# One written order for the whole kernel: q and k as nine tokens a partition, PSUM banks as single tiles, weight loads held to a place in the order

## The chip, the cores and the metric

The kernel runs on one core of a Trainium2 chip, in one launch. The metric is device time in microseconds (us). The kernel computes with TensorE (PE: matmuls and transposes, weight loads shown as PEld), VectorE (DVE), ScalarE (ACT) and GpSimd (POOL). DMAs are issued by SyncE's queue (SP), by POOL (where float32 is cast to fp16 on the way) and a few by ACT. Each engine and each queue takes its instructions strictly in program order.

## What is computed

There are 8 batches of 8 heads with 576 tokens of 64 channels. Each head has a coarse attention (q, k and v averaged over 4 tokens, 144 by 144 scores, output repeated 4 times) and a local one (each token sees the keys less than 4 tokens away). Their sum goes, as 4608 tokens by 512 channels, through a two-layer MLP with an ELU:

```python
out_up = np.repeat(out_d, factor, axis=2)            # coarse attention, factor 4
mask = np.abs(pos[:, None] - pos[None, :]) < factor  # local attention
out_local = np.matmul(attn, v)
x = (out_up + out_local) ...                         # [B * S, H * D] = [4608, 512]
h = x @ w_in                                         # 512 -> 2048
g = np.where(h > 0.0, h, np.exp(np.minimum(h, 0.0)) - 1.0)
return g @ w_out                                     # 2048 -> 512
```

## The kernel before

Attention goes by pairs of heads, 4 pairs (j) in each of 8 batches (b). The MLP goes by 9 blocks (t) of 512 tokens; a block has 64 matmuls of 128x512 for the first layer (`mm1`: 16 columns of blocks fc, 4 matmuls dc each, where dc is the pair of heads whose channels it reads) and 64 for the second (`mm2`). Block t needs the attention of batches up to t for t of 1 to 7, and block 0 needs batch 0 alone. So the kernel is a front (batch 0, the weights, batch 1), a long middle in which a batch of attention is worked in between the matmuls of the MLP, and an end of MLP alone.

- Loads: `load_qk` brings q and k of a pair as float32 on SP, on 96 partitions with 6 tokens each (two runs of 1536 bytes a partition); `load_cast` does it for batches 0 and 1 on POOL's queue. `load_v`/`load_windows` (L258, L280) bring v, from batch 1 on as four DMAs of 80 KB a pair in pieces of 256 bytes, into one of 3 buffers. `load_wi` (L172) and `load_wo` (L176) bring the weights in four DMAs each on POOL's queue.
- `cast_qk` (L242) and `cast_v` (L303) cast to fp16 on POOL. `transposes` (L324, L329) turn q, and in batches 0 to 2 k, by six transposes of 96x128 a tensor; from batch 3 on (`FLIP`) a DMA transpose turns k (L808). `evict_q`/`evict_k` (L359, L366) put the tokens in order; `sums` (L378 on DVE, L395 and L397 on POOL) makes the coarse q and k.
- `scores` and `coarse` (L459, L472), `exps` (L482), `mask` (L497), `denominators` (L519, L525); the reciprocals are spread over partitions by PE and a copy (L582, L592) in batches 0 to 2, and through DRAM after (`spread_out`, `spread_in`); `near_outputs`, `far_outputs` (L603, L623), `normalise` (L667, L672, L684).
- Batch 0 has a program of its own (`masked_scores`, `masked_exps`, `den_half`, `spread_half`, `outputs_half`, `normalise_half`): windows of 112 keys, a mask that is added through PE, coarse sums through PE, work in half batches. The first layer of block 0 runs in halves of 256 tokens (`mm1_part`, L699).
- `mm1` (L720), then `exp` on ACT (L724), `min(e,1)-1` (L725) and `max(h,0)+e` (L726) on DVE; `mm2` (L740), a copy on ACT (L746) and a store on SP (L748).
- PSUM has eight banks: two tiles of two banks for scores, outputs, spreads and transposes (a third one until `close_front`), two banks for `mm1`, two for the rest. `keep` issues idle matmuls on a zero tile (L759).

The order is a list of events sorted by a time written out by hand, in units of about one `mm1` column; all engines get their instructions in that one order. The numbers for the front stand in `F`, those for the batches in `PLAN`, and `MM1`/`MM2` place the MLP:

```python
for _, _, fn, args in sorted(events, key=lambda e: e[:2]):
    fn(*args)
```

Of the kernel before, what the change touches and what calls it, by code (L numbers as in the profile page):

```python
# [16 lines left out]
SD = S // 4  # L17
SH = SD // 2
SCALE = 0.125
QB, KW, NB, PAD = 96, 112, 6, 8  # L20
HB = 3 * QB
TPP = S // QB
# [5 lines left out]
RW = S + SD  # L28
KG, CG = 96, 24
KO = 16  # L30
# [5 lines left out]
I1 = 31  # L36


def _np_consts():

    f16 = np.float16
    off = np.arange(KW) - PAD
    m = np.zeros((KW, NB, QB), dtype=f16)
    for c in range(NB):
        for u in range(QB):
            ok = (np.abs(off - u) < 4) & (off + QB * c >= 0) & (off + QB * c < S)
            m[ok, c, u] = 1.0
    m = m.reshape(KW, S)
    neg = ((m - 1) * 30000).astype(f16)
    rs = np.zeros((QB, 3, SD), dtype=f16)  # L50
    for c in range(3):
        rs[np.arange(QB), c, (TPP * np.arange(QB) + 2 * c) // 4] = 0.25
    vr = np.zeros((KW, 32), dtype=f16)
    vr[PAD + np.arange(QB), np.arange(QB) // 4] = 0.25
    ind = np.zeros((KW, 190), dtype=f16)
    ind[:, I1] = 1.0
    ind[np.arange(KW) % 32 < CG, 63 + I1] = 1.0
    ind[:, 126:] = 1.0
    for n, z in enumerate((10, 5)):
        ind[:, 127 + 32 * n : 126 + 32 * n + z] = 0.0  # L60
    return np.eye(KW, dtype=f16), neg, rs.reshape(QB, 3 * SD), vr, ind


def _np_windows():
# [26 lines left out]
    return mask.reshape(128, WL), vr.reshape(128, 96), ind  # L91
# [12 lines left out]
def kernel(  # L104
# [11 lines left out]
    dr = ctx.enter_context(tc.tile_pool(name="dr", bufs=1, space=bass.MemoryType.DRAM))  # L116
    ctx.enter_context(nc.allow_low_precision("fp16 operands of TensorE"))
    ctx.enter_context(tc.manual_schedule())

    def const(a, name, queue):  # L120
        t = C[name] = sb.tile(list(a.shape), FP16, tag=name, bufs=1, name=name)
        queue.dma_start(out=t[:], in_=nc.inline_tensor(a, name=name + "c").ap())

    front = ctx.enter_context(ExitStack())
    ps = ctx.enter_context(tc.tile_pool(name="ps", bufs=1, space=bass.MemoryType.PSUM))
    fp = front.enter_context(tc.tile_pool(name="fp", bufs=1, space=bass.MemoryType.PSUM))
    late = {}

    def one(name, dt=FP32):
        return ps.tile([128, 512 if dt == FP32 else 1024], dt, tag="misc", bufs=2, name=name)  # L130

    turns = [0, 1, 2]

    def two(name, dt=FP32):

        turns.append(turns.pop(0))
        pool = fp if turns[-1] == 2 else ps
        return pool.tile([128, 1024 if dt == FP32 else 2048], dt, tag=f"two{turns[-1]}", bufs=1, name=name)

    def bank(tag, name):  # L140
        pool = late["ps"] if tag == "hp" else ps
        return pool.tile([128, 512], FP32, tag=tag, bufs=2, name=name)

    def close_front():
        front.close()
        turns.remove(2)
        late["ps"] = ctx.enter_context(
            tc.tile_pool(name="late", bufs=1, space=bass.MemoryType.PSUM)
        )

    def g2(ap, a, n):

        return _free(ap[:, a : a + 1], [[512, 2], [1, n]])
# [4 lines left out]
    id_np, neg_np, sums_np, vr_np, ind_np = _np_consts()  # L158
    mask_np, vr2_np, ind2_np = _np_windows()
    C = {}  # L160
    WI = sb.tile([128, DMC, DFF], FP16, tag="WI", bufs=1, name="WI")
    WO = sb.tile([128, FCN, DM], FP16, tag="WO", bufs=1, name="WO")
    KT = [sb.tile([128, S + 2 * KO], FP16, tag=f"kt{i}", bufs=1, name="kt") for i in range(4)]

    def w_in(dc, fc):

        a = 512 * (fc // 4) + fc % 4
        return WI[:, dc, a : a + 509 : 4]

    def load_wi(a, z):  # L170
        src = moe_w_in.rearrange("(c p) m -> p c m", p=128)[:, :, a:z]
        nc.gpsimd.dma_start(out=WI[:, :, a:z], in_=src)  # L172

    def load_wo(n):
        src = moe_w_out[512 * n : 512 * n + 512].rearrange("(p c) m -> p c m", c=4)
        nc.gpsimd.dma_start(out=WO[:, 4 * n : 4 * n + 4, :], in_=src)  # L176

    KD = [sb.tile([128, 2 * KG + 16], FP16, tag=f"kd{i}", bufs=1, name="kd") for i in range(4)]
    KE = [sb.tile([128, 192], FP16, tag=f"ke{i}", bufs=1, name="ke") for i in range(4)]
    QT = [sb.tile([128, S + 4], FP16, tag=f"qt{i}", bufs=1, name="qt") for i in range(4)]  # L180
    qk32, qk16, v32s, v16s = {}, {}, {}, {}
    st = {}

    def runs_of(src, b, j):

        a = src[b, 2 * j]
        return bass.AP(
            tensor=a.tensor, offset=a.offset, ap=[[TPP * D, QB], [S * D, 2], [1, TPP * D]]
        )

    def by_head(x):

        return x[:].rearrange("p c e d -> p (c e d)").rearrange("p (e n) -> p e n", e=2)

    def is_cast(b, j):

        return b < 2 and (b, j) != (0, 0)

    def load_cast(b, j):
        qk16[(b, j)] = []  # L200
        for src, name in ((q, "q16"), (k, "k16")):
            x = sb.tile([QB, NB, 2, D], FP16, tag=name, bufs=4, name=name)
            nc.gpsimd.dma_start(out=by_head(x), in_=runs_of(src, b, j))
            qk16[(b, j)].append(x)

    def load_qk(b, j, held=False):

        got = []
        for src, name in ((q, "q"), (k, "k")):
            a = src[b, 2 * j]  # L210
            t = sb.tile([QB, 2 * NB, D], FP32, tag=name + "32", bufs=3, name=name + "32")
            if held:
                nc.vector.memset(t[0:1, 0, 0:1], 0.0)
            runs_ = name == "q" or b < FLIP
            nc.sync.dma_start(
                out=t[:].rearrange("p (e r) d -> p e (r d)", e=2) if runs_ else t[:],
                in_=bass.AP(
                    tensor=a.tensor, offset=a.offset,
                    ap=[[TPP * D, QB], [S * D, 2], [1, TPP * D]] if runs_
                    else [[D, QB], [QB * D, 2 * NB], [1, D]],  # L220
                ),
            )
            got.append(t)
        qk32[(b, j)] = got

    AP_ = sb.tile([1, 1], FP16, tag="apart", bufs=1, name="apart")

    def apart(x):

        nc.gpsimd.tensor_copy(out=AP_[:], in_=x)  # L230

    def cast_qk(b, j, half=False):

        got = []
        for t, name in list(zip(qk32.pop((b, j)), ("q16", "k16")))[:: 1 if b < FLIP else -1]:
            x = sb.tile([QB, NB, 2, D], FP16, tag=name, bufs=4, name=name)
            src = t[:].rearrange("p (e c) d -> p c e d", e=2)
            if half:
                act(out=x[:, :, 0, :], in_=src[:, :, 0, :])
                dve(out=x[:, :, 1, :], in_=src[:, :, 1, :])  # L240
            else:
                nc.gpsimd.tensor_copy(out=x[:], in_=src)  # L242
                apart(x[0:1, 0, 0, 0:1])
            got.append(x)
        qk16[(b, j)] = got[:: 1 if b < FLIP else -1]

    V00 = sb.tile([KW, 2 * NB, D], FP32, tag="v32", bufs=3, name="v32")

    def load_v(b, j):

        a = v[b, 2 * j]
        if b:
            load_windows(b, j, a)
            return
        t = V00 if (b, j) == (0, 0) else sb.tile([KW, 2 * NB, D], FP32, tag="v32", bufs=3, name="v32")

        def part(p0, p1, i0, i1):
            nc.sync.dma_start(  # L258
                out=t[p0:p1, i0:i1, :],
                in_=bass.AP(  # L260
                    tensor=a.tensor, offset=a.offset + (QB * i0 - PAD + p0) * D,
                    ap=[[D, p1 - p0], [QB * D, i1 - i0], [1, D]],
                ),
            )

        if (b, j) == (0, 0):
            part(0, KW, 1, 2 * NB)
            part(PAD, KW, 0, 1)
        else:
            part(0, KW, 0, 2 * NB)  # L270
        v32s[(b, j)] = t

    def load_windows(b, j, a):

        t = sb.tile([128, 2 * WM, D], FP32, tag="v32", bufs=3, name="v32")
        if b == 1:
            nc.vector.memset(t[0:1, 1, 0:1], 0.0)

        def part(h, e, n=64, m0=0, m1=WM):
            nc.sync.dma_start(  # L280
                out=t[64 * h : 64 * h + n, WM * e + m0 : WM * e + m1, :],
                in_=bass.AP(
                    tensor=a.tensor, offset=a.offset + (WQ * h - 3 + S * e + 2 * WQ * m0) * D,
                    ap=[[D, n], [2 * WQ * D, m1 - m0], [1, D]],
                ),
            )

        last = (b, j) == (B - 1, NPAIR - 1)
        if last:
            nc.gpsimd.memset(t[96:128, 2 * WM - 1, :], 0.0)  # L290
# [756 lines left out]
```

## Time and profile before

| what | value |
| --- | --- |
| runs (3) | 350.78 us median, 350.11 to 354.14 |
| profiled execution, first to last instruction | 355.1 us |
| PE busy / weight loads | 336.1 / 185.5 us |
| DVE, ACT, POOL busy | 236.4, 180.3, 160.8 us |
| mean granted TensorE clock | 0.976 |
| HBM read, written | 41.97 MB, 9.55 MB |

The profiled execution is a little longer than the three timed runs. PE's busy time counts overlapping matmuls and PE's waits inside a pipelined group too, so it is not PE at its peak; what an instruction really takes of PE is read from the distance of its start to the next one's. The granted clock is the share of the full TensorE clock. DMA shares are sums of the times of packets over 16 engines, and can exceed 1 where packets overlap.

### The profile page before, as it was taken

To read this page: it belongs to the slowest core of one execution; us is meant where nothing else is said; L and a number is where in the kernel's file an instruction comes from. 1 tells how busy PE (TensorE), PEld (TensorE's weight loads), DVE (VectorE), ACT (ScalarE), POOL (GpSimd) and SP (SyncE) were. 2 spreads that over 40 slices of the span, in tenths; PEclk is the share of its full clock that TensorE was granted. 3 is DMA by queue.
4 is the path that set the end of the run, shared out by engine and by line. 5 is a ranking of instruction groups with operands and counts; after the bars stand their busy time and mean duration, and the time that the engine had idled before them with its cause. 6 is when DMAs were issued, how large, how long until landed. Compare 5 with 4: busy or idle time off the path is not lost.

```text
span 355.1 us, 10487 instructions
## 1 busy us (share of the span) xinstructions
PE 336.1 (95%) x4288; PEld 185.5 (52%) x4288; DVE 236.4 (67%) x466; ACT 180.3 (51%) x312; POOL 160.8 (45%) x298
## 2 busy tenths in 40 slices
PE   7993998799979999999999999999999999999996
PEld 3762885344545454545454555555455544444443
DVE  2334799566789877987697789768755855555510
ACT  4580587225755664466456645663553444444421
POOL 4464449279495834974397449855300500000000
PEclk9998799959999999999999999999999999999999
DMA  8999979997999698998979796943004010011012
GB/s 173 184 166 203 191 172 216 215 186 185 189 152 224 120 205 168 167 185 174 181 155 206 158 218 144 188 123 61 30 32 118 31 59 30 31 46 43 31 59 89
DMA packets 100304, 48.89 MB, mean 138 GB/s; under 512 B 81617, under 2 KB 95265, under 8 KB 100257
## 3 DMA queue, kind: packets, MB, share of 16 engines
q1 hardware_dynamic: 94417, 41.86, 57.8%
q0 software_dynamic: 5600, 6.26, 10.8%
q8 instruction: 33, 0.54, 0.7%
q10 hardware_dynamic: 240, 0.11, 0.2%
q14 instruction: 14, 0.11, 0.1%
HBM read 41.97 MB, written 9.55 MB: 145 GB/s over the span
## 4 chain that ended last, share of the span: by engine, by line
PE 72%; DMA 13%; DVE 6%; ACT 3%; issue 2%; POOL 2%; SPq 1%; DVEq 0%; POOLq 0%; ACTq 0%
PE op L740 31%; PE hp L720 28%; DMA v<-in_v_dram 6%; DMA rcb<-rd 3%; DMA WO<-in_moe_w_out_dram 3%; DVE ln L672 2%; PE sc L759 2%; PE tqk L329 2%; DMA rd<-rc 2%; PE lg L603 2%; DVE e L725 1%; PE sc L459 1%; ACT e L724 1%; DVE gt L726 1%; PE lg L623 1%
## 5 line engine op out<-in xcount | busy, mean ns | idle before, releaser
L740 PE MATMUL op<-WO,gt 128*128 128x512 f16 (+2 forms) x592 | 147.0, 377 | 1.0 <-DVE gt L726 0.6
L724 ACT ACTIVATE e<-hp 128x512 f16<-128x512 f32 x144 | 86.1, 599 | 110.5 <-PE hp L720 95.7
L720 PE MATMUL hp<-xt,WI 128*128 128x512 f16 x512 | 133.4, 384 | 0.7 <-DVE gt L726 0.5
L726 DVE SCALAR_TENSOR_TENSOR gt<-hp,e 128x512 f16<-128x512 f32 x144 | 99.6, 692 | 6.4
L725 DVE TENSOR_SCALAR e<-e 128x512 f16<-128x512 f16 x144 | 60.7, 421 | 58.1 <-ACT e L724 57.6
L740 PEld LDWEIGHTS <-gt 128*128 128x128 f16 x592 | 55.6, 98 | 62.8 <-issue 3.0
L720 PEld LDWEIGHTS <-WI 128*128 128x128 f16 x512 | 55.5, 115 | 49.6 <-issue 3.1
L684 POOL TENSOR_TENSOR xt<-ln 128x128 f16<-128x128 f16 (+7 forms) x55 | 36.7, 695 | 50.8 <-DVE ln L672 50.8
L482 ACT ACTIVATE pex<-sc 128x580 f16<-128x580 f32 (+1 forms) x56 | 30.2, 596 | 9.7 <-PE sc L472 9.7
L395 POOL TENSOR_TENSOR t<-qt 128x288 f32<-128x288 f16 x27 | 18.1, 671 | 36.8 <-ACT qt L359 36.8
L303 POOL CAST v<-v 128x640 f16<-128x640 f32 (+1 forms) x32 | 24.2, 756 | 21.1 <-DMA v<-in_v_dram 21.0
L746 ACT COPY os<-op 128x512 f32<-128x512 f32 (+2 forms) x37 | 21.4, 577 | 19.3 <-PE op L740 19.1
L378 DVE TENSOR_REDUCE ke<-kt 128x145 f16<-128x580 f16 x28 | 21.0, 751 | 2.4 <-ACT kt L366 2.4
L359 ACT COPY qt<-tqk 128x576 f16<-128x576 f16 x28 | 17.9, 638 | 8.5 <-PE tqk L329 6.7
L699 PE MATMUL hp<-xt,WI 128*128 128x256 f16 x128 | 17.3, 288 | 4.6 <-issue 4.6
L672 DVE TENSOR_TENSOR ln<-lg,rcb 128x580 f16<-128x580 f32 x28 | 21.1, 752 | 0.0
L242 POOL CAST q<-q 96x768 f16<-96x768 f32 x24 | 19.9, 828 | 0.0
L242 POOL CAST k<-k 96x768 f16<-96x768 f32 x24 | 19.8, 825 | 0.1
L699 PEld LDWEIGHTS <-WI 128*128 128x128 f16 x128 | 13.6, 118 | 5.8 <-issue 4.7
L497 DVE TENSOR_TENSOR pex<-pex,MASK 128x580 f16<-128x580 f16 x28 | 14.0, 500 | 3.8 <-ACT pex L482 3.6
L397 POOL TENSOR_TENSOR qd<-t 128x144 f16<-128x144 f32 x27 | 12.4, 461 | 2.1
L459 PEld LDWEIGHTS <-kt 64*64 64x64 f16 x560 | 7.0, 108 | 11.7 <-issue 8.8
(113 smaller groups left out, 271.6 us busy)
## 6 DMA issues: line engine op xcount, KB each, us to landing
out_dram<-os SPq DMA_DIRECT2D x35, 256.0 KB, 2.2
v<-in_v_dram SPq DMA_DIRECT2D x111, 80.0 KB, 4.6
q<-in_q_dram SPq DMA_DIRECT2D x25, 288.0 KB, 4.1
k<-in_k_dram SPq DMA_DIRECT2D x25, 288.0 KB, 5.1
rcb<-rd SPq DMA_DIRECT2D x10, 364.0 KB, 4.6
WI<-in_moe_w_in_dram POOLq DMA_DIRECT2D x4, 512.0 KB, 10.9
WO<-in_moe_w_out_dram POOLq DMA_DIRECT2D x4, 512.0 KB, 9.2
q<-in_q_dram POOLq DMA_DIRECT2D x7, 144.0 KB, 7.2
```

The lines of the kernel that those rows point to most:

```text
L242: nc.gpsimd.tensor_copy(out=x[:], in_=src)
L303: nc.gpsimd.tensor_copy(out=v16[:], in_=v32[:].rearrange("p (e c) d -> p c e d", e=2))
L482: nc.scalar.activation(out=s["p"][:, :, a : a + n], in_=g2(sc, a, n), func=AF.Exp, scale=SCALE / 16 if a else SCALE,)
L672: nc.vector.tensor_tensor(out=ln[:, 0 : 2 * WL].rearrange("p (m h u) -> p m h u", h=2, u=WQ), in0=_free(lg[:, 0:1], [[WQ, WM], [512, 2], [ ...
L684: eng.tensor_tensor(out=xt(t)[:, j, t0 - TBLK * t : t1 - TBLK * t], in0=ln[:, a:z], in1=_rep4(ln[:, ga : ga + (z - a) // 4]), op=AB.add,)
L699: nc.tensor.matmul(FS[i][:, 256 * f : 256 * f + 256], w_in(dc, 2 * n + f), xts[0][:, dc, 256 * h : 256 * h + 256], start=(f == dc == 0), s ...
L720: nc.tensor.matmul(hp, w_in(dc, fc), xts[t][:, dc, :], start=(dc == 0), stop=(dc == DMC - 1),)
L724: nc.scalar.activation(out=e, in_=hp, func=AF.Exp)
L725: nc.vector.tensor_scalar(out=e, in0=e, scalar1=1.0, scalar2=-1.0, op0=AB.min, op1=AB.add)
L726: nc.vector.scalar_tensor_tensor(out=to, in0=hp, scalar=0.0, op0=AB.max, in1=e, op1=AB.add)
L740: nc.tensor.matmul(op_[:, a:z], gts[t][:, fc, 128 * tt : 128 * tt + 128], WO[:, fc, a:z], start=(fc == 0), stop=(fc == FCN - 1),)
L746: nc.scalar.copy(out=os_[:, a:z], in_=op_[:, a:z])
```

## The change

The program is written anew. The order of everything is one string of 1730 words (`ORDER`), made by a list scheduler, and a word is a step with its numbers: which tensor, batch, pair, the engine (0 ACT, 1 DVE, 2 POOL, 4 SP) or the PSUM tile. All batches take the same path, so batch 0's own functions, their constants and the fourth kind of window go. In particular:

- q, and k where PE turns it, are loaded as one run of nine tokens (2304 bytes) on each of 128 partitions, and turned by 18 transposes of 64x64 a tensor (`t`) in place of six of 96x128. k by DMA transpose (`fl`) is as before.
- The four single PSUM banks (4 to 7) are tiles of their own, and any of them serves `mm1`, `mm2`, a turn, the v sums or the denominators as the order says; two tiles of two banks stay, the third is there until `close`.
- `min(e,1)` and `max(e-1, h)` replace `min(e,1)-1` and `max(h,0)+e`; in 28 of 144 columns ACT does the minimum by itself (`er` relu(-h), `ey` exp(-e)). 24 of the final adds (`ad`) go to DVE, most sums of k (`s.1`) go to POOL.
- `WI` is two tiles, loaded in four parts (half the columns, two dc each), `WO` four. `hw` writes one element of a weight tile on DVE, so that the load of it waits for that place in DVE's order; `hv` and `hx` do the same for the first loads of v, q and k into a buffer. v has 4 float32 buffers instead of 3.
- The first layer of block 0 runs over all 512 tokens, matmul by matmul as a pair is ready (`m.t.fc.d0.d1.bank`).

```diff
+    def load_x(x, b, j, eng):
+        src = bass.AP(tensor=a.tensor, offset=a.offset, ap=[[NINE * D, 128], [1, NINE * D]])
...
+    def hold_w(n, eng):
+        engines[eng].memset((WI[0][0:1, 0, 0:1], WO[0][0:1, 0, 0:1])[n], 0.0)
...
+    def load_wi(n, i, eng):
+        src = moe_w_in.rearrange("(c p) m -> p c m", p=128)
+        queues[eng].dma_start(
+            out=WI[n][:, 2 * i : 2 * i + 2, :], in_=src[:, 2 * i : 2 * i + 2, 1024 * n : 1024 * n + 1024]
+        )
...
+    def turn(x, b, j, p):
+        src, to = nth((Q16, K16)[x], b, j), bank(p).bitcast(FP16)
+        for c in range(NINE):
+            for e in range(2):
+                r = heads(e)
+                nc.tensor.transpose(to[r, 64 * c : 64 * c + 64], src[r, 64 * c : 64 * c + 64], ID[r, r])
...
+    def elu_min(t, fc, eng):
+        e = e_of(t, fc)
+        engines[eng].tensor_scalar(out=e, in0=e, scalar1=1.0, scalar2=None, op0=AB.min)
...
+    for word in ORDER.split():
+        name, *numbers = word.split(".")
+        STEPS[name](*map(int, numbers))
```

Words of `ORDER` that the prediction speaks of, in their order (`...` where words are left out; `lv` v load, `lx` q or k load, `cx`, `cv` casts, `e` copy of a turn, `sc` scores, `x` exps, `mk` mask, `vs`, `vc` sums of v, `dn`, `rc`, `sp`, `sy` denominators to their spread, `ne`, `fa`, `n`, `ad` outputs to the MLP's input, `w` mm2, `r`, `st` its copy and store):

```text
... s.0.0.1.2 ... s.1.0.1.2 ... s.0.0.2.2 ... mk.0.1.2 ... cv.0.0.2 ... cv.0.1.2 ... dn.0.0.2.5 hw.0.1 s.1.0.3.2 ...
wi.0.0.2 ... sc.0.3.0 lv.1.1.0.4 ... wi.0.1.2 ... wi.1.0.2 ... wi.1.1.2 ... n.0.2.0 n.0.3.1 ad.0.2.0.2
lv.1.2.1.4 ad.0.3.1.1 ad.0.3.0.2 warm.12.5 m.0.0.2.3.6 lx.0.1.3.2 m.0.1.0.1.7 warm.1.5 m.0.0.3.4.6 ...
t.0.1.0.4 ... hw.1.1 ... cv.1.0.2 ... wo.0.2 ... wo.1.2 ... cv.1.1.2 ... wo.2.2 ... wo.3.2 ... w.0.0.0.4.0.512.7 ...
w.0.0.8.12.0.512.7 ... w.0.0.12.16.0.512.7 ... t.0.2.2.5 ... sc.2.2.0 ... m.1.0.0.4.7 ...
```

More of the change, by code (lines that the diff above doesn't have):

```diff
@@ L35 @@
 FLIP = 3
-I1 = 31
-def _np_consts():
[L41 to L61, printed above, removed]
@@ L132 @@
[L132 to L144, printed above, removed]
-        front.close()
[L146 to L149, printed above, removed]
+    PB.append(psum(fp, 2, 1024, "pb"))
@@ new lines, in close, with bank @@
+    def close():
+        front.close()
+        late = ctx.enter_context(tc.tile_pool(name="late", bufs=1, space=bass.MemoryType.PSUM))
+        for i in (6, 7):
+            ONE[i] = psum(late, i, 512, "one")
+    def bank(n):
+        return ONE[n][:]
+    id_np, con_np = _np_consts()
+    ID = keep("ID", [128, 128])[0]
+    CON = keep("CON", list(con_np.shape))[0]
+    VR2, IND, MASK = CON[:, 0:96], CON[:, 96:269], CON[:, 269 : 269 + WL]
+    FOUR = keep("FOUR", [128, 1024])[0]
+    I4 = keep("I4", [128, 16])[0]
@@ L228, in apart, with load_wo @@
+    def load_wo(n, eng):
+        src = moe_w_out[512 * n : 512 * n + 512].rearrange("(p c) m -> p c m", c=4)
+        queues[eng].dma_start(out=WO[n][:], in_=src)
     def apart(x):
         nc.gpsimd.tensor_copy(out=AP_[:], in_=x)
[L232 to L245, printed above, removed]
@@ L273, in load_windows @@
[L273 to L290, printed above, removed]
-        for h in range(2):
-            for e in range(2):
-                if last and h == e == 1:
-                    part(1, 1, m1=WM - 1)
-                    part(1, 1, S + 3 - 9 * WQ, WM - 1)
-                else:
-                    part(h, e)
-        v32s[(b, j)] = t
@@ L509, in denominators @@
+    def denominators(b, g0, g1, p):
+        den = bank(p)
         steps = []
@@ L882, in first_outputs @@
-    def first_outputs(i, n):
-        lg = FS[(i, 2)] = two("lg")
-        keep(lg, n)
-        outputs_half(*halves(i), lg)
-    def first_normalise(i):
-        normalise_half(*halves(i), FS.pop((i, 2)))
-    def ahead(dc):
-        for i in range(2):
-            for f in range(2):
-                mm1_part(i, f, dc)
-    events = []
-    def at(time, fn, *args):
-        events.append((time, len(events), fn, args))
-    def pair_scores(b, j):
-        sc = two("sc")
-        scores(j, sc)
-        coarse(b, j, sc)
-        exps(b, j, sc, 0, WL)
-        exps(b, j, sc, WL, SD + SH)
-        mask(b, j)
@@ new lines, in os_of, with result, store @@
+    def os_of(t, tt):
+        return OS[(4 * t + tt) % 4]
+    def result(t, tt, a, z, p, eng):
+        copies[eng](out=os_of(t, tt)[:, a:z], in_=bank(p)[:, a:z])
+    def store(t, tt, a, z):
+        r = TBLK * t + 128 * tt
+        nc.sync.dma_start(out=out[r : r + 128, a:z], in_=os_of(t, tt)[:, a:z])
+    STEPS = dict(
+        id=c_id, con=c_con, zeros=zeros, four=four, warm=warm, lx=load_x, hx=hold_x, hv=hold_v, hw=hold_w, close=close, lv=load_v,
+        zv=zero_v, wi=load_wi, wo=load_wo, cx=cast_x, cv=cast_v, t=turn, fl=flip, e=turned, s=sums,
+        sc=scores, x=exps, mk=mask, vs=v_sums, vc=v_copy, dn=denominators, rc=reciprocals,
+        so=spread_out, si=spread_in, sp=spread, sy=spread_copy, ne=near, fa=far, n=normalise, ad=add,
+        m=mm1, ex=elu_exp, em=elu_min, er=elu_relu, ey=elu_exp2, eg=elu_max,
+        w=mm2, r=result, st=store,
+    )
```

1063 lines of the change are left out of this document (431 added, 632 removed).

## The prediction

> **What bounds the kernel now.** I read the page first, then stretches of the span (a table by windows), the matmuls of the MLP in the same stretches, the chain that ended last, and last the single rows of PE and of the DMA queues. The page says that PE is the bound over the whole:
>
> ```profile
> span 355.1 us, 10487 instructions
> PE 336.1 (95%) x4288; PEld 185.5 (52%) x4288; DVE 236.4 (67%) x466; ACT 180.3 (51%) x312; POOL 160.8 (45%) x298
> ```
>
> That is an average over stages. By stretches (PE, PEld, DVE, ACT, POOL busy, then granted clock, DMA share, GB/s):
>
> ```profile
> 0.00:28.00 28.00, 24.48 (x480) 16.32 (x481) 9.30 (x40) 16.10 (x27) 13.87 (x23) 1.00 1.00 175
> 28.00:40.00 12.00, 7.35 (x108) 5.56 (x107) 5.09 (x9) 1.84 (x3) 5.84 (x10) 0.72 1.28 204
> 40.00:58.00 18.00, 17.31 (x307) 15.12 (x302) 16.81 (x38) 15.61 (x29) 11.14 (x22) 1.00 0.95 191
> 58.00:76.20 18.20, 14.71 (x309) 8.57 (x307) 11.35 (x24) 5.86 (x10) 9.12 (x17) 0.84 1.10 202
> 83.30:113.00 29.70, 26.95 (x483) 15.19 (x481) 24.10 (x43) 19.09 (x35) 19.82 (x40) 1.00 1.03 185
> 113.00:281.00 168.00, 166.95 (x2248) 86.60 (x2247) 131.79 (x243) 90.64 (x158) 92.62 (x175) 1.00 0.72 144
> ```
>
> From 113 us on PE is busy 166.95 of 168.00 us at full clock: there only work that PE does not have to do can be won. What can be won lies before. Of the MLP this is done by 83.3 us (the same windows with the instructions of one line; first the half-size first layer of block 0, L699, then L740, then L720):
>
> ```profile
> 28.00:40.00 12.00, 3.55 (x16) 1.93 (x16) 0.72 1.28 204
> 40.00:58.00 18.00, 13.75 (x112) 11.65 (x112) 1.00 0.95 191
> ...
> 58.00:76.20 18.20, 7.04 (x24) 2.12 (x24) 0.84 1.10 202
> 76.20:83.30 7.10, 2.95 (x9) 1.10 (x10) 0.68 0.80 188
> ...
> 76.20:83.30 7.10, 4.39 (x12) 1.41 (x12) 0.68 0.80 188
> ```
>
> That is 128 halves (64 full ones), 33 of the second layer and 12 of block 1: 109 of 1152 (one more starts just before 76.2). The chain and PE's rows say why so few:
>
> ```profile
> 25.70 11.13 DMA v<-in_v_dram
> 36.84 8.99 DMA v<-in_v_dram
> ...
> 55.32 10.15 DMA WO<-in_moe_w_out_dram
> 65.51 1.02 PE op L740 x4
> ...
> 34.28 1.02 PE L699 MATMUL hp<-xt,WI 128*128 128x256 f16 x4 [4.65 <-issue]
> 40.06 2.15 PE L699 MATMUL hp<-xt,WI 128*128 128x256 f16 x18
> ```
>
> PE stands 4.65 us for the weights at 34.28; the bulk of block 0 starts at 40.06; v of batch 1 waits for a free buffer and the queue, and the last quarter of WO, issued by POOL only at 55.32 behind casts, lands at 65.5. Each wait also costs clock (0.72, 0.84).
>
> **The front up to block 0.** In the new order the last engine ready for `m.0.0.2.3` is POOL. Its rows:
>
> ```profile
> 8.93 0.45 PE L324 MATMUL tq<-ID,q 96*64 96x96 f16 x12 [1.08 <-ACT qd L848]
> L395 POOL TENSOR_TENSOR t<-qt 128x288 f32<-128x288 f16 x27 | 18.1, 671 | 36.8 <-ACT qt L359 36.8
> L397 POOL TENSOR_TENSOR qd<-t 128x144 f16<-128x144 f32 x27 | 12.4, 461 | 2.1
> L303 POOL CAST v<-v 128x640 f16<-128x640 f32 x28 | 20.8, 744 | 12.3 <-DMA v<-in_v_dram 12.3
> L497 DVE TENSOR_TENSOR pex<-pex,MASK 128x580 f16<-128x580 f16 x28 | 14.0, 500 | 3.8 <-ACT pex L482 3.6
> L684 POOL TENSOR_TENSOR xt<-ln 128x512 f16<-128x512 f16 x4 | 4.3, 1068 | 0.0
> L203 POOL DMA_DIRECT2D q<-in_q_dram x7 | 4.7, 665 | 1.2 <-POOLq L1031 0.9 <-issue 0.3
> L172 POOL DMA_DIRECT2D WI<-in_moe_w_in_dram x4: 750/752/767, 16.9 to 20.6; - x4
> WI<-in_moe_w_in_dram POOLq DMA_DIRECT2D x4, 512.0 KB, 10.9
> ```
>
> Its first sum can begin where pair 1 is turned today, 8.93. Behind it stand four sums of 0.67 + 0.46 (4.5), the mask of one pair, two v casts (1.5), four WI issues (3.0), six q and k issues at 0.66 (4.0), three adds of 512 columns (3.2) and two of 64, which I estimate at 0.3 from the same row (0.6). A mask of 128x580 is not shown on POOL. Bounds are 0.5, as DVE takes for it, and 1.3, the 512-wide add scaled up; it is an operation of POOL, so I take 1.2. In all 18.0, to 26.9 us. WI agrees: `hw` and the sums let it go at about 16.5, today it goes at 16.9, and 10.9 us to landing makes 27.4 to 27.8. So block 0 starts its bulk at about 27.5 in place of 40.06. The float32 casts that this shortens and the functions of batch 0 that go have their price in this; they are hidden behind POOL's list.
>
> **From there to block 1.** From `m.0.0.3` to `m.1.0` the order gives PE 107 full matmuls and the attention around them. The prices are distances between starts:
>
> ```profile
> 91.19 0.42 PE L329 MATMUL tqk<-ID,q 96*128 96x96 f16 x6
> 91.70 1.03 PE L720 MATMUL hp<-xt,WI 128*128 128x512 f16 x4
> 92.57 1.03 PE L740 MATMUL op<-WO,gt 128*128 128x512 f16 x4
> ...
> 94.56 1.03 PE L740 MATMUL op<-WO,gt 128*128 128x512 f16 x4
> 95.51 0.35 PE L459 MATMUL sc<-qt,kt 64*64 64x58 f16 x20
> 95.90 1.04 PE L740 MATMUL op<-WO,gt 128*128 128x512 f16 x4
> ...
> L726 DVE SCALAR_TENSOR_TENSOR gt<-hp,e 128x512 f16<-128x512 f32 x144 | 99.6, 692 | 6.4
> L725 DVE TENSOR_SCALAR e<-e 128x512 f16<-128x512 f16 x144 | 60.7, 421 | 58.1 <-ACT e L724 57.6
> ```
>
> Four full matmuls take 0.87; a turn of six takes half of 91.19 to 91.70, 0.26; the scores of a pair take 0.39; and a full group before 64x64 work takes 0.95, so each change to small tiles costs about 0.1 more. 107 matmuls at 0.216 are 23.1. 16 turns at 0.45 (see below) are 7.2, five scores 2.0; spreads, outputs, denominators and sums of v, some 13 groups that I price like scores, 5.1; more switches 1.4. PE's sum is 38.8. DVE has 16 columns at 0.69 and 15 at 0.42, that is 17.4, and 28 instructions of the attention at its mean of 0.51 (236.4 by 466), 14.3, together 32: close behind PE, so I add 5 us of waits (bounds 2 and 12). 27.5 + 38.8 + 5 = 71.3 us at `m.1.0`, with 112 matmuls of the MLP done. Today 109 are done at 83.3: **12 us** ahead. In attention the new order stands four turns and a score further, 2 us more. A part of the 12 is the clock: at 0.84 of 18.2 and 0.68 of 7.1 us today loses about 5 us, and that goes with the waits.
>
> **What it adds after.** The turn is not shown: 18 transposes of 64x64, two at a time. Lower bound: 0.26, as six of 96x96; upper: 20 products of 64x58 with their successors, 0.39, and the switch of 0.1, that is 0.5. It is nearest to the 64x64 row; I take 0.45 alone, less where turns stand together. 20 turns of q remain after block 1: 0 to 4.8, taken 3 us lost. DVE gives 28 minima to ACT (11.8 us) and takes 24 adds and some copies, ACT takes 56 passes for the 28; both are hidden by PE in the stretch from 113 to 281, where DVE has 131.79 and ACT 90.64 of 168, and if that cover went, a batch would be longer by what one of them has above 34 us. The new POOL and SP orders are dense while PE works batches 2 to 4; I take 3 us lost there in waits that the 29.70 us stretch does not show yet (bounds 0 and 15, the latter the rival below). The end is as before: a last block of the second layer, a copy, a store.
>
> Sum: -12 - 2 + 3 + 3 = **8 us less** than the profile's 355.1, so 347.1 in a profiled execution. The median of the runs is 350.8 (this profile was 1.2% longer than it), and the same difference gives **342.8 us**. A change of 2%, 7 us, is about what a measurement of this kernel tells from none.
>
> **Rivals.** *Nothing lost after* (12%): the turns hide as they did and the waits are those of today; -14 plus 1, so 337.8.
>
> *Held weights come late again* (18%). The two queues share the DMA engines, and between 24 and 34 us their packets went one for one, those of POOL's queue (q0) at nearly four times the size:
>
> ```profile
> q0 software_dynamic: 1634, 1.52, 90.7%
> q1 hardware_dynamic: 1668, 0.41, 31.3%
> ```
>
> WI in larger packets and casts in larger packets give v of batch 1 fewer turns, an 80 KB load being 320 packets of 256 bytes. `wo.2` and `wo.3` stand on POOL behind `cv.1.1`, which needs the eighth of these loads. If the eighth lands 7 us after the place the order gives it, block 1 starts at 78, 7 of the gain go: 350. For it: the 11.13 us of a v load in the chain. Against: WI and the casts also finish sooner. [...]
>
> *SP becomes the bound* (slower, 16%). The order brings all loads before block 4, so SP is fuller than today:
>
> ```profile
> L280 SPq DMA_DIRECT2D v<-in_v_dram x113: 428/619/1947, 17.1 to 227.1; - x113
> L808 SPq DMA_TRANSPOSE kt<-k x20: 1222/1250/2114, 88.6 to 236.7; - x20
> ```
>
> Between `m.2.0` and `m.3.0` SP issues 25 v loads (15.5), 6 transposes (7.5) and 22 other DMAs, which I put at no more than a v load (13.6): 36.6 us beside 38.8 of PE. If a v issue takes 0.9, between its median and its longest, it is 44, and stores stand behind loads: output tiles come free late, ACT's copy waits, and so does PE's bank. From where SP's list passes PE's, each of the three stages of blocks 1 to 3 loses its 5 us: 342.8 + 15 = 358.
>
> *The clock falls in the front* (2%): eight turns of small transposes a batch stand there, and some 10 us of PE's work before `m.0.0.2.3` would take twice the time, 353. Against it: the front of today, with its transposes and small matmuls, holds a clock of 1.00 for 28 us. [...]
>
> *The order does not do what it says* (2%): v, q, k and weights land as today whatever is held, and the front ends at 40: 350.
>
> **How the numbers follow.** Forecast 50%, own range 338 to 347, of which 36 points lie under 343.8 (2% less) and 14 over. Nothing lost after 12%, all under. Late weights 18%, fallen clock 2% and no effect 2% lie within 2%; of these 2 points I count as slower. SP 16%, over 357.8. Faster 0.48, same 0.34, slower 0.18. The range is 334 (waits at their lower bound 2, turns free, nothing lost after) to 357 (late weights and half of SP's loss).
>
> **What would show it.** Right: `mm1` of block 0 from near 27 us without long pauses, block 1 near 71, no stretch at half clock after 20 us, 18 transposes taking 0.35 to 0.5 of PE, and PE nearly closed behind `m.1.0`. Wrong: PE waiting for WO or for v of batch 1 between 45 and 65; idle time of ACT's result copies ended by SP's stores; turns over 0.6 each; gaps of PE spread over 75 to 180 us.

## The result, and the profile after

The changed kernel takes **365.41 us** (median of 4 runs, 363.18 to 368.49) against 351.7 us of the kernel before beside it: a ratio of **1.042, 95% interval 1.032 to 1.052**. Run again later it gave 1.037 (1.030 to 1.045). It is slower by some 4%; the forecast was 342.8 us. All ratios are of fast executions alone, but the profiles of the changed kernel again, of POOL's sum ahead of casts and of k in larger pieces are of slow ones. The profile of the kernel before is a long one too: 43 of its 46 later timed executions span less than its 355.1 us. The page of the profiled execution (TensorE, its clock and the DMA engines in 40 slices of 9.13 us):

```profile
span 365.3 us, 11074 instructions
...
PE 335.1 (92%) x4593; PEld 174.8 (48%) x4593; DVE 238.6 (65%) x469; ACT 190.7 (52%) x332; POOL 157.6 (43%) x293
...
PE   8879989979995899497979899999999999999995
...
PEclk9866999999996999899999999999999999999999
DMA  8799799799989699999699954140004000100112
...
DMA packets 95628, 48.62 MB, mean 133 GB/s; under 512 B 80986, under 2 KB 85722, under 8 KB 95578
```

PE has the same busy time as before (335.1 and 336.1) in a span 10 us longer. The slices of PE below 9 that are new lie between 110 and 210 us, and the DMA row is nearly full until the same place. By stretches, the changed kernel:

```profile
83.30:113.00 29.70, 25.54 (x409) 13.44 (x408) 20.83 (x39) 15.72 (x27) 19.12 (x39) 0.97 0.97 164
113.00:150.00 37.00, 33.25 (x400) 16.54 (x400) 22.37 (x36) 19.57 (x34) 21.46 (x45) 0.93 1.00 195
150.00:193.00 43.00, 35.43 (x602) 19.02 (x602) 34.00 (x56) 23.75 (x42) 24.73 (x47) 0.93 1.01 191
```

and the kernel before in the last two of them:

```profile
113.00:150.00 37.00, 36.67 (x487) 19.08 (x486) 29.72 (x56) 20.77 (x37) 24.40 (x45) 1.00 0.89 167
150.00:193.00 43.00, 42.33 (x561) 21.84 (x559) 34.10 (x62) 24.07 (x44) 27.29 (x54) 1.00 0.91 175
```

Where before loses 1 us of 80, the changed kernel loses 11.3, and 7% of its clock besides. The start of the n-th matmul of the MLP (the rows of its two lines counted in order of time; a half counts half) shows when. The last three columns are experiments below.

| n of 1152 | before | after | after, small loads | after, k in larger pieces | before, small loads |
|---|---|---|---|---|---|
| 10 | 40.4 | 36.0 | 39.1 | 43.8 | 38.4 |
| 190 | 113.4 | 98.1 | 100.2 | 104.3 | 108.3 |
| 250 | 129.8 | 123.0 | 118.2 | 123.0 | 124.8 |
| 370 | 161.6 | 162.1 | 151.1 | 157.7 | 156.4 |
| 550 | 209.7 | 218.6 | 202.9 | 214.2 | 203.5 |
| 910 | 299.6 | 308.8 | 292.7 | 303.9 | 293.4 |

At 98 us the changed kernel is **15.3 us ahead**, at 219 us **9 us behind**, and then nothing changes any more: 24 us are lost in 120. The loss is firmer than the lead: from start 190 to 910 the kernel before takes 186 us (185 in the two profiles of it with changed loads, below) and the changed one 211, while the front differs by several us from one profile to the next. The waits of PE in 95 to 215 us and the chain at the longest pause:

```profile
PE pb L512 <- DVE ln L641: 7.8, 4, 5.0
PE pb L521 <- POOL qd L503: 4.2, 1, 4.2
PE one L545 <- DVE gt L684: 3.0, 2, 1.6
```

```profile
143.59 0.62 SPq L413
144.21 0.04 issue
144.26 0.62 SPq L584
144.88 0.04 issue
144.92 6.73 DMA rcb<-rd
...
151.78 0.10 DVE ln L636
...
152.00 0.76 DVE ln L641
152.76 0.04 issue
152.81 0.20 PE pb L512
```

The reciprocals of batch 3 (L584) go out behind seven loads of v on SP's queue and need 6.73 us to land. The other long pause, with what follows it on PE:

```profile
108.78 0.35 PE L512 MATMUL pb<-qt,kt 64*64 64x58 f16 x20
113.36 0.40 PE L521 MATMUL pb<-qd,ke 64*64 64x144 f16 x8 [4.23 <-POOL qd L503]
...
114.14 4.80 PE L662 MATMUL one<-xt,WI 128*128 128x512 f16 x12
```

A sum of q on POOL stood behind casts of batch 4 that waited for their loads. Twelve matmuls then take 4.6 us instead of 2.6: the granted clock is 0.50 between 112 and 118 us, at the end of this pause of 4.2 us and behind it. It is also 0.50 from 190.0 to 193.3 us, behind a pause of 2.1; how long a pause it takes for that is not shown.

### The profile page after: what moved, and what is told of

It is laid out like the page before. It is cut to its first block, busy times and chain, and to the rows that moved or that the text cites. A ratio compares the mean times of both kernels' runs of the same rounds, so it can differ in the third digit from the quotient of the medians.

```text
span 365.3 us, 11074 instructions
## 1 busy us (share of the span) xinstructions
PE 335.1 (92%) x4593; PEld 174.8 (48%) x4593; DVE 238.6 (65%) x469; ACT 190.7 (52%) x332; POOL 157.6 (43%) x293
## 3 DMA queue, kind: packets, MB, share of 16 engines
q1 hardware_dynamic: 91610, 41.48, 53.3%
## 4 chain that ended last, share of the span: by engine, by line
PE 50%; DMA 20%; SPq 12%; DVE 8%; POOL 5%; issue 2%; ACT 1%; POOLq 0%; DVEq 0%; ACTq 0%
PE one L690 22%; PE one L662 20%; SPq L413 9%; DMA v<-in_v_dram 8%; DMA rcb<-rd 5%; DMA q<-in_q_dram 3%; DMA kt<-k 2%; POOL v L461 2%; DVE ln L641 2%; PE one L377 2%; DVE gt L684 1%; DVE pn L536 1%; SPq L474 1%; PE one L471 1%; POOL t L499 1%
## 5 line engine op out<-in xcount | busy, mean ns | idle before, releaser
L662 PE MATMUL one<-xt,WI 128*128 128x512 f16 x576 | 142.5, 385 | 2.6 <-DVE gt L684 1.8
L690 PE MATMUL one<-WO,gt 128*128 128x512 f16 (+2 forms) x592 | 141.5, 378 | 0.0
L684 DVE SCALAR_TENSOR_TENSOR gt<-e,one 128x512 f16<-128x512 f16 x144 | 98.2, 686 | 11.4 <-ACT e L681 5.9
L671 ACT ACTIVATE e<-one 128x512 f16<-128x512 f32 x116 | 69.4, 598 | 68.6 <-PE one L662 50.0
L652 POOL TENSOR_TENSOR xt<-ln 128x64 f16<-128x64 f16 (+7 forms) x40 | 28.6, 729 | 47.9 <-DVE ln L641 44.9
L699 ACT COPY os<-one 128x512 f32<-128x512 f32 (+1 forms) x35 | 20.4, 581 | 36.8 <-PE one L690 36.8
L528 ACT ACTIVATE pn<-pb 128x580 f16<-128x580 f32 x32 | 20.5, 661 | 22.3 <-PE pb L521 22.2
L461 POOL CAST v<-v 128x640 f16<-128x640 f32 x29 | 21.5, 743 | 13.0 <-PE pb L612 8.2
L641 DVE TENSOR_TENSOR ln<-pb,rcb 128x580 f16<-128x580 f32 x32 | 24.0, 751 | 0.0
L536 DVE TENSOR_TENSOR pn<-pn,CON 128x580 f16<-128x580 f16 x27 | 18.4, 691 | 6.8 <-ACT pn L528 6.8
L678 ACT ACTIVATE e<-one 128x512 f16<-128x512 f32 x28 | 16.8, 599 | 10.2 <-PE one L662 8.2
L636 DVE TENSOR_TENSOR ln<-pb,rcb 128x144 f16<-128x144 f32 x32 | 9.6, 301 | 18.4 <-DMA rcb<-rd 9.6
L455 POOL CAST q<-q 128x576 f16<-128x576 f32 x22 | 14.5, 660 | 10.8 <-PE one L471 5.6
## 6 DMA issues: line engine op xcount, KB each, us to landing
WI<-in_moe_w_in_dram POOLq DMA_DIRECT2D x4, 512.0 KB, 10.8
```

Source lines behind the costliest of these rows:

```text
L461: copies[eng](out=t[:], in_=nth(V32, b, j)[:].rearrange("p (e c) d -> p c e d", e=2))
L528: nc.scalar.activation(out=nth((PN, PF)[n], b, j)[:], in_=g2(PB[p], a, w), func=AF.Exp, scale=SCALE / 16 if a else SCALE,)
L536: engines[eng].tensor_tensor(out=to, in0=to, in1=mk2, op=AB.mult)
L641: nc.vector.tensor_tensor(out=ln[:, 0 : 2 * WL].rearrange("p (m h u) -> p m h u", h=2, u=WQ), in0=_free(lg[:, 0:1], [[WQ, WM], [512, 2], [ ...
L652: engines[eng].tensor_tensor(out=XT[t % 3][:, j, t0 - TBLK * t : t1 - TBLK * t].rearrange("p (u f) -> p u f", f=4), in0=ln[:, a:z].rearran ...
L662: nc.tensor.matmul(bank(p), WI[n][:, dc, a : a + 509 : 4], XT[t % 3][:, dc, :], start=(dc == 0), stop=(dc == DMC - 1),)
```

## Experiments

All ratios are to the kernel before on the same chip. In the diffs words of `ORDER` stand without their last numbers.

**The changed kernel again.** 

> The changed kernel once more, unaltered, beside the variants. All theories: 1.03 to 1.05 of the kernel before. In the profiles so far the last v of batch 0 lands at 24.1 us (twice) or at 28.9 to 29.9 (twice) and the bulk of block 0 starts at 34.3 to 34.9 or 38.2 to 39.7 accordingly, with the same lists up to there: if that is chance between WI's and v's transfers, this profile shows one of the two again.

1.037 (1.030 to 1.045). The last v of batch 0 was cast at 28.1 us and the bulk of block 0 started at 39.1.

**Reciprocals first.**
```
- rc.3 st.1.2 so.3 lx.1.6.0 lv.5.0.2 lv.5.0.3 lv.5.3.0 lv.5.3.1 lv.5.3.2 lv.5.3.3 lv.5.1.0 si.3.0 si.3.1
+ rc.3 so.3 lx.0.5.1 lx.1.5.2 lx.0.5.2 lv.5.0.0 lv.5.0.1 lx.1.5.3 st.1.2 si.3.0 si.3.1
```
(batch 4 likewise) 

> SyncE's list alone is changed: the store and the spread loads of the reciprocals of batches 3 and 4 (so, si) go to the place right behind their reciprocal, ahead of nine loads of q, k and v that stood before them. No DMA is added or left out. Theory Q (the loss between 107 and 211 us is made by loads that run ahead and stand in in-order lists before what TensorE needs): rcb of batch 3 lands near 145 instead of 151.7, TensorE's pause of 5.3 us at 145.9 and the half clock after it go, that of 2.5 us at 185.6 too: 365.4 - 8 to 10 = 356 to 358. Theory B (the DMA engines are full, whoever is first): another transfer is late by the same time, 363 to 366. Theory P (TensorE's own list is wrong whatever the DMAs do): 364 to 366, the pause only moves.

1.043 (1.033 to 1.054): nothing gained. Its waits of PE in the same stretch:

```profile
PE pb L519 <- POOL qd L501: 4.5, 1, 4.5
PE one L660 <- POOL xt L650: 4.2, 1, 4.2
PE one L660 <- DVE gt L682: 2.2, 1, 2.2
```

The pause at 146 is gone, and a new one stands at 158, where an add of POOL is queued behind the cast of a late q.

**POOL's sum ahead of casts.**
```
- cx.1.4.0 cx.0.4.0 cx.1.4.1 s.0.3.1 ad.2.2.2 cx.1.4.2 ad.2.3.3
+ s.0.3.1 ad.2.2.2 ad.2.3.3 cx.1.4.0 cx.0.4.0 cx.1.4.1 cx.1.4.2
```


> GpSimd's list alone is changed: the casts of q and k of batch 4 (cx.1.4.0, cx.0.4.0, cx.1.4.1, cx.1.4.2) go behind the sum of q of pair 1 of batch 3 (s.0.3.1) and two adds of block 2 (ad.2.2.2, ad.2.3.3), which stood behind them. Theory Q: the pause of 4.4 us at 108.8 (the score of that pair waits for qd) and the half clock from 114.1 to 118.8 (2.3 us) go: 365.4 - 5 to 7 = 358 to 360. Theory B: the loads for which GpSimd waited are late for the next user, 363 to 366. Theory P: 364 to 366.

1.040 (1.030 to 1.050), but this tells nothing: two of the casts came to stand behind the next loads into their own buffers and waited for those (a pause of 8.7 us at 118). The sum is moved properly in the next one.

**Five places at once.** The moves of the first experiment, and
```
+ e.0.3.1 s.0.3.1 cx.0.4.0;  ad.2.2.2 ad.2.3.3 cx.1.4.1;  ad.3.2.3 ad.3.3.4 cx.0.5.3 cv.5.1 cv.5.3
+ cx.0.5.0 lx.0.5.3 lv.5.1.1 lv.5.1.2 lv.5.1.3 lv.5.2.0 lv.5.2.1
```


> Lists alone are changed, in five places at once, since a single place gave nothing (the pause came back at the next one): so and si of batches 3 and 4 as before; on GpSimd the sum of q s.0.3.1 ahead of the cast cx.0.4.0 (in a place where its buffer allows it), two adds of block 2 ahead of the cast cx.1.4.1, two adds of block 3 ahead of the casts cx.0.5.3, cv.5.1, cv.5.3; on SyncE the load of q of the last pair of batch 5 ahead of five loads of v. No DMA is added or left out. Theory Q (in-order lists with loads that run ahead): the pauses at 108, 120, 146 and 158 go together, ratio to the kernel before 1.00 to 1.02 (350 to 358). Theory B (DMA engines full): the pauses move on, 1.035 to 1.05. Theory D (Vector and GpSimd have too much in these 100 us): 1.035 to 1.05 as well, with pauses ended by DVE at the same sums.

1.033 (1.024 to 1.042). With its profile 8.8 us ahead of before at the first block, it ends 5.6 behind. Between 107 and 211 us, the five places moved and then the changed kernel as it is:

```profile
107.00:211.00 104.00, 88.23 (x1304) 45.48 (x1305) 69.35 (x123) 54.85 (x98) 59.75 (x118) 0.93 0.95 188
```

```profile
107.00:211.00 104.00, 87.22 (x1280) 44.78 (x1279) 70.97 (x119) 51.98 (x92) 59.98 (x119) 0.93 1.00 193
```

The moves win 1 us of the 17 that PE is idle here. The theory that these places in the lists are the cause falls.

**v later.** All `lv` and `cv` of batches 3 to 7 go back by up to 60 or 110 words (most by about 52 or 95). The edit moves one thing more: five groups of idle matmuls (`warm`) leave their places in the front and stand with later ones just ahead of and in block 0, so the ratios are not those of a later v alone. 

> All loads of v of batches 3 to 7 and their casts go 60 places (some 11 us) back in the order, each still ahead of its first use; nothing else is changed, no DMA added or left out. In the changed kernel v is cast 35 to 45 us before the sums of v read it. Theory R (v running ahead fills the DMA engines just when q, k, the flips and the reciprocals are urgent): those land in 2 to 5 us in place of 5 to 8, half to two thirds of the 16 us that small loads gave back come back: ratio 1.005 to 1.02. Theory B (the engines' time for this volume is the limit, whatever the order): 1.03 to 1.045.

> The same with 110 places (some 20 us). Theory R: 1.00 to 1.015, the loads end near 230 us as in the kernel before instead of 213. Theory B: 1.03 to 1.045. If v then comes too late itself, a pause at the casts of v (GpSimd) and the sums of v: 1.04 or more, less good than 60 places.

1.044 (1.033 to 1.055) and 1.043 (1.032 to 1.054). With 110 words the last v is issued at 237 us instead of 213, and the window from 107 to 211 us loses idle time (11 us instead of 17) while the first block started 6 us later than before in this profile, with the idle matmuls out of place:

```profile
107.00:211.00 104.00, 92.79 (x1381) 48.21 (x1380) 71.73 (x127) 54.75 (x96) 61.59 (x121) 0.93 1.04 191
```

The DMA engines are as full as they were (1.04 and 1.00). From start 190 to 550 this kernel takes 114.4 us, 6 less than the changed kernel. So these two runs don't show that a v that runs ahead costs nothing; they speak for a part of the loss.

**v of batches 4 to 7 small.**
```
+        if b >= 4:
+            part(0, 64, 0, 1)
```


> Every load of v of batches 4 to 7 moves only the first of its five windows (64 packets of 256 bytes instead of 320), so those batches are computed with old values in the other windows; the number of DMAs, all lists and all waits stay. 4.1 of 48.6 MB and some 16,000 of 95,600 packets are gone, nearly all of them between 108 and 208 us. Theory B (volume): the loss of 22 us between 107 and 211 goes nearly whole, 345 to 350. Theory Q (places in the lists): SyncE still needs 0.62 us for each and si still stands behind them; only the time to land gets shorter (rcb from 6.7 to some 3 us, twice): 356 to 361. Theory P: 363 to 366.

1.021 (1.012 to 1.030): some 2% of the 4 come back. That is the upper end of theory Q's range and far from what theory B said for volume. With the DMA share down to 0.81 between 107 and 211 us, PE still idles for 11 of the 104 us there.

**Small loads.**
```
+        if b >= 3:                      # load_v
+            part(0, 64, 0, 1)
...
+        if b >= 4:                      # load_x: 64 of 576 columns
+            queues[eng].dma_start(out=t[:, 0:D], ...)
```


> The loads are made small with lists, waits and the number of DMAs unchanged: v from batch 3 on brings one of five windows, q and k from batch 4 on bring 64 of 576 columns, so these batches are computed with old values elsewhere. The share of the DMA engines between 107 and 211 us falls from 0.97 to some 0.4. Theory B: the 22 us lost there come back nearly whole, ratio 0.98 to 0.99 (343 to 348). Theory Q: landings get short (2 to 3 us in place of 5 to 8), so that lists hardly wait: half to two thirds come back, 1.00 to 1.01. Theory D (engines too full whatever the DMAs do): 1.03 to 1.04.

**0.990 (0.984 to 0.996).** Same lists, same number of DMAs, and the loss is gone, as theory B had it. The window from 107 to 211 us of this kernel:

```profile
107.00:211.00 104.00, 99.80 (x1577) 52.59 (x1576) 85.55 (x148) 65.19 (x116) 69.15 (x138) 1.00 0.44 92
```

**k in larger pieces.**
```
-        if x == 1 and flipped(b):       # load_x
-            src = ...[[D, QB], [QB * D, 2 * NB], [1, D]]
```


> The loads of k of batches 3 to 7 bring the same bytes in 128 pieces of 2304 bytes in place of 1152 of 256 bytes (nine tokens a partition); casts, transposing DMAs and lists stay, so k of these batches stands in a wrong order for the flips. Some 20,000 of 95,600 packets go, no byte does, TensorE gets no work. Three memsets in the front fill columns that the casts read. Theory B-packets: the DMA share between 107 and 211 us falls from 0.97 to about 0.75 and 8 to 13 of the 22 us come back: ratio 1.00 to 1.015. Theory B-bytes: 1.03 to 1.045.

**1.012 (1.002 to 1.023)**, about two thirds of the loss, with every byte still moved; the interval leaves anything from some 40% of it to nearly all. Its page:

```profile
DMA packets 75148, 48.62 MB, mean 135 GB/s; under 512 B 57946, under 2 KB 62682, under 8 KB 75098
...
q1 hardware_dynamic: 71130, 41.48, 48.3%
```

The same row of the changed kernel:

```profile
q1 hardware_dynamic: 91610, 41.48, 53.3%
```

53.3% of 365.3 less 48.3% of 360.4, times 16 engines, is 330 us of engine time for 20,480 packets: some 16 ns each, an estimate from these two rows. At equal bytes the changed kernel takes less with these packets gone, 1.012 against 1.037 and 1.042; what one packet of 256 bytes costs by itself is not shown.

**k turned by TensorE.** `FLIP = 8`, and for each `fl.b.j` a `t.1.b.j e.1.b.j`. 

> k of batches 3 to 7 comes like k of the first three: nine tokens a partition (128 pieces of 2304 bytes in place of 1152 of 256 bytes) and turned by TensorE, 20 turns and 20 copies in place of 20 transposing DMAs; bytes moved stay nearly the same, some 20,000 of 95,600 packets go. Theory B in the form that packets cost, not bytes: the DMA share between 107 and 211 us falls from 0.97 to 0.7 to 0.8 and the pauses shrink by 12 to 16 us, against 20 turns at 0.45 (9 us) where they stand alone: ratio 1.00 to 1.025. If bytes are the limit or the lists: 1.04 to 1.065, the turns come on top.

> As the run with k of batches 3 to 7 turned by TensorE, the turns now in banks that have been free for longer and are wanted again later, and so and si of batches 3 and 4 moved up as in the first experiment. If packets are the limit: the bank waits of some 10 us in that run fall to 3 and the reciprocals come in time: ratio 1.01 to 1.025. If they are not: 1.035 or more.

> The same with all five moves of the lists (sums and adds on GpSimd ahead of casts, a load of q ahead of loads of v). If with room on the DMA engines the lists' places count: 3 to 6 us less than e13_turnk_si, 1.00 to 1.015. If they never counted: the same as it within 1%.

1.040 (1.030 to 1.050), 1.025 (1.016 to 1.033), 1.026 (1.018 to 1.034). The DMA share between 107 and 211 us falls to 0.67, but the turns take back on PE what the packets gave, and in the first of them PE also waited some 11 us for banks that the turned copies held. The second run changes the turns' banks and the places of the reciprocals together, so what either is worth is not shown. The other four moves still count for nothing with room on the DMA engines (1.025 and 1.026). None of these beats the kernel before.

**The same two edits in the kernel before.**
```
-            runs_ = name == "q" or b < FLIP
+            runs_ = True
```


> The kernel before with k of batches 3 to 7 in pieces of 1536 bytes (192 a load in place of 1152 of 256 bytes), as q and the first batches have it; casts, transposing DMAs and order stay, so k of these batches stands in a wrong order for the flips. Some 19,000 of 100,300 packets go, no byte does. If the changed kernel alone stands against the loads (its TensorE came 13 us earlier to where they set the pace): TensorE was closed here from 113 us on, 0.99 to 1.005 of the kernel before. If the packets cost any order the same: 0.97 to 0.98, as the changed kernel gained.

> The kernel before with the small loads: v from batch 3 on brings one of five windows, q and k from batch 4 on 64 columns; these batches are computed with old values elsewhere, and the tiles of the loads are kept instead of allocated anew. If the changed kernel alone stands against the loads: only its pauses between 83 and 113 us (2.75 us) and 1 us later can go, 0.985 to 1.00. If loads cost any order the same: 0.95 to 0.965.

**1.001 (0.997 to 1.005) and 0.997 (0.993 to 1.000).** The kernel before does not feel its loads, as its windows from 107 to 211 us say, first as it is and then with small loads:

```profile
107.00:211.00 104.00, 102.50 (x1500) 53.62 (x1500) 83.31 (x154) 58.40 (x102) 61.77 (x117) 1.00 0.93 179
```

```profile
107.00:211.00 104.00, 103.82 (x1434) 54.17 (x1433) 84.53 (x155) 57.63 (x101) 64.91 (x123) 1.00 0.37 83
```

That is the control: it is not the packets alone that cost, but that the changed kernel has come to where loads set the pace.

**The front.** Half of v of batch 0 on ACT's queue (`lv.0.j.2.0`, `lv.0.j.3.0` behind `con.0`): 

> Half of the loads of v of batch 0 (the second head of each pair, eight of 17 DMAs) is issued by ScalarE's queue right behind its constants, the others by SyncE as before. Theory F (the bulk of block 0 waited for the last v of batch 0, which SyncE issued only at 17.0 us because 17 issues of 0.62 us and more stand in one list): the last v lands near 17 instead of 24.1, WI's half by 27.2 as before, and the bulk of block 0 starts near 28 instead of 34.9: the end is 3 to 6 us earlier, 359.5 to 362.5. If the transfers and not the issues were the limit: the last v still lands at 22 to 24, 364 to 366. If GpSimd's list were the last, as the prediction had it: no change, 364 to 366.

1.053 (1.044 to 1.062). The last v did land at 17.4 us as expected, but ACT stood in its own issues until 14.1, and the first sum on POOL began at 16.2 us instead of 7.5; the bulk started at 39.9. Second half of WI and three loads behind `ad.0.1.0`, then the first v of batch 1 behind `ad.0.0.0` as well: 

> GpSimd's list alone is changed: the second half of WI (wi.1.0, wi.1.1) and the first three casting loads of batch 1 are issued behind the add ad.0.1.0 (near 22 us) instead of ahead of it (18.1 to 21 us). Theory F2 (these transfers take the DMA engines from the last v of batch 0, which near and far of pairs 2 and 3 wait for): that v lands at 20 to 22 in place of 24 or 29, TensorE's pause of 2.5 to 8.5 us at 21.4 is gone and the bulk of block 0 starts at 30 to 32: ratio 1.02 to 1.03. If only the order of landings changes and block 0 then waits for WI: 1.035 to 1.045, with a pause at 45 us for WI's second half.

> As in the last expectation (second half of WI and three loads of batch 1 behind the add ad.0.1.0), and the first eight loads of v of batch 1 are held behind the add ad.0.0.0 (near 24 us) too, so that between 17.6 and 22 us only the first half of WI shares the DMA engines with the last v of batch 0. Theory F3 (whatever transfers stand behind it delay that v, by chance from 20 to 29 us): it lands at 20 to 22 and the bulk of block 0 starts at 30 to 31.5; some 4 of these 8 us are lost again where v of batch 1 is late: ratio 1.015 to 1.03. If its landing does not depend on what is issued behind it: bulk at 34 to 40, 1.035 to 1.05.

1.043 (1.036 to 1.049) and 1.041 (1.034 to 1.048). The last v of batch 0 was cast at 28.4 and 28.1 us, the bulk started at 38.9 and 39.5: fewer transfers behind that v did not bring its landing forward.

## Why the prediction was wrong, by its own steps

**What bounds the kernel** was read rightly as to PE. But the DMA share of 1.00, 1.28, 0.95, 1.10 and 1.03 stood in the same rows, and I used it only for who comes first. By 83.3 us the two kernels have moved 15.8 and 15.9 MB (190 and 191 GB/s), by 113 us 21.3 and 20.8, by 150 us 27.5 and 28.0 (from the windows' last column):

```profile
0.00:83.30 83.30, 70.96 (x1221) 48.65 (x1222) 46.51 (x113) 42.98 (x75) 46.38 (x83) 0.90 1.04 190
```

```profile
0.00:83.30 83.30, 74.23 (x1442) 40.79 (x1443) 54.98 (x133) 47.69 (x84) 53.27 (x96) 0.92 0.94 191
```

The change brings PE forward by 15 us and no byte: loads that were hidden before are not hidden any more. The same from start 190 to 550 of the MLP, before and then after:

```profile
113.40:209.70 96.30, 95.30 (x1308) 49.46 (x1307) 75.73 (x140) 53.83 (x95) 57.20 (x110) 1.00 0.90 175
```

```profile
98.10:218.60 120.50, 103.48 (x1557) 53.58 (x1556) 83.09 (x143) 62.51 (x110) 68.83 (x135) 0.94 0.94 184
```

Between the same two marks the changed kernel moves 22.2 MB where the kernel before moves 16.9. Of the 5.3 MB more, 3.2 have not yet been moved at the first mark, and 2.1 come ahead of where the kernel before has them. At 184 GB/s they are 17 and 11 us. That is a reckoning and no test, but it fits the lead that goes and the 9 us behind, and in the run with 110 words, which has moved 1.0 MB less at the second mark, the 6 us that this stretch got shorter.

**The front, 27.5 for the bulk of block 0**, was wrong: 34.9 here, 30.6 to 42.7 in ten other profiles with the same order up to there. POOL's list did what was said (WI issued from 16.6, 10.8 us to landing; a mask 1.15 where 1.2 was taken):

```profile
L435 POOL DMA_DIRECT2D WI<-in_moe_w_in_dram x4: 728/737/772, 16.6 to 18.8; - x4
...
L536 POOL TENSOR_TENSOR pn<-pn,CON x5: 1142/1154/1199, 11.7 to 259.9; 128x580 f16<-128x580 f16 x5
```

The engine that is ready last is not POOL but SP: 17 issues of v at 0.62 us and more, the last at 17.02, landed 7.1 us later. In all eleven profiles the bulk starts 10.0 to 11.5 us after this landing, which itself lies anywhere from 19.9 to 31.2:

```profile
22.46 0.33 PE L628 MATMUL pb<-pf,vd 128*64 128x72 f16 x4
24.99 0.30 PE L545 MATMUL one<-v,CON 128*32 128x128 f16 x8 [2.20 <-ACT v L461]
...
30.37 4.02 PE L377 MATMUL one<-Z 128*128 128x512 f16 x12
34.23 0.59 PE L662 MATMUL one<-xt,WI 128*128 128x512 f16 x2
```

Twelve fillers (L377) then stand ahead of the bulk for 4 us, most of them at half clock (0.50 from 27.0 to 32.9 us).

**From there to block 1** came out close. PE's sum was 38.8 for the stretch; it is busy 38.71, and 41 us pass where 43.8 were given:

```profile
34.20:76.00 41.80, 38.71 (x774) 21.80 (x773) 31.38 (x69) 27.87 (x50) 23.98 (x44) 1.00 0.91 196
```

Block 1 starts at 76.0 instead of 71.3; the 12 to 14 us ahead were there, 15.3, at 98 us. But some 5 us of this lead were chance in the profile of before. In the profile of its run with k in larger pieces, where the first altered load goes out at 68 us, start 64 is at 52.5 instead of 57.6 and start 109 at 76.9 instead of 83.3. The sum took a gain that held against a long execution off the median of the runs.

**What it adds after** holds the failed step. The turn was close: 0.45 taken; the row has 0.47, and 0.40 pass from its start to that of the group after it:

```profile
168.41 0.47 PE one L471 x18
```

"3 us lost in waits" (bounds 0 and 15), with 3 more for the turns, measured 24. With small loads the changed kernel goes from 13.2 ahead to 6.9 ahead (from 8.1 to 0.7 against the kernel before with small loads), so 6 or 7 us are the turns and dense orders, as the sum had it (3 + 3). The other 18 are the price of loads that set the pace, a term the sum did not have. Even without them the forecast gain of 8 us is not there: the two kernels with small loads have 0.990 (0.984 to 0.996) and 0.997 (0.993 to 1.000), which overlap. The front came 7 us later than forecast, and some of the lead had been read off a long profile.

**The rivals.** "SP becomes the bound" had the sign, the place (blocks 1 to 3), 15 us, and perhaps more. No output tile was late, and other places in SP's list gave nothing. But between `m.2.0` and `m.3.0` SP's issues, added up from the trace, take 44.8 of 47.8 us (forecast 36.6, or 44 with slow issues), partly because there are 59 in place of 53, partly because v and the transposing DMAs issue more slowly (0.72 and 1.65 each, where 0.62 and 1.25 were taken). From start 190 to 550 they take 110 of 120 us, and with small loads 88 of 103 for nearly as many. So small loads relieve the engines and SP's queue together, and no run here tells the two apart. Held weights were not late: PE does not wait for WO. The clock did fall in the front, to 0.80 of 34 us, but behind pauses of 1.6 and 2.2 us (0.50 from 16 to 22 and from 27.0 to 32.9); the stretch from 34 to 76 us, quoted above, has 1.00 with twice as many turns in it (16 and 8), so that turns lower the clock is not shown:

```profile
0.00:34.20 34.20, 28.22 (x529) 15.01 (x530) 16.50 (x50) 13.10 (x21) 22.53 (x41) 0.80 0.93 171
```

**What stays open:** why the last v of batch 0 lands between 20 and 31 us when it is issued at 16.0 to 18.4; whether the DMA engines or SP's issues are the tighter of the two between 98 and 219 us; and how much of the loss a v that keeps its later place would save, as the bytes suggest. A part of the 24 us is the half clock after pauses: 7% of 87 us, 6 us, between 107 and 211.

## What to carry to other kernels

A lead won by order holds only as far as the data come: before you book it, add up the bytes, the small packets and the issues of each queue between two marks of the work, and compare them with the DMA share and the queue's time in the stretches that lie before. Take the base of a forecast from a profile as long as the median of the runs. When moving a waiting instruction only moves the pause, test the resource behind it: make the transfers small with lists and waits unchanged, and make the same edit in the kernel before as a control. Packets of 256 bytes are worth counting apart from bytes: 20,480 packets fewer at the same bytes took the changed kernel from 1.042 and 1.037 to 1.012, while some 19,000 fewer left the kernel before at 1.001.

## What was not expected of the hardware

A mask on DVE takes 0.46 us when POOL is idle and up to 1.69 beside POOL's casts and adds. Not every one beside POOL is slow: half of the 27 take 0.46 or less, most of them beside some work of POOL. Here two take 2.15 us while POOL adds and casts:

```profile
114.49 2.15 DVE L536 TENSOR_TENSOR pn<-pn,CON 128x580 f16<-128x580 f16 x2 [5.53 <-ACT pn L528]
...
115.20 0.51 POOL L652 TENSOR_TENSOR xt<-ln 128x192 f16<-128x192 f16 x1
...
115.66 0.66 POOL L455 CAST q<-q 128x576 f16<-128x576 f32 x1
```

```profile
L536 DVE TENSOR_TENSOR pn<-pn,CON x27: 446/464/1686, 13.7 to 268.2; 128x580 f16<-128x580 f16 x27
```
